# Spreading the first layer norm over the engines, and its side work over ticks, in a four-layer attention kernel

## The chip, the cores and the metric

The kernel runs on one core of one Trainium2 chip. The metric is device time in microseconds (us) of one execution. A kernel is timed several times in alternation with the kernel before on the same chip; medians are quoted ("same": within 2%).

TensorE does matmuls, ScalarE (ACT in the profile) the exps, VectorE (DVE) the masks, evictions and statistics, GpSimd (POOL) small work and stores, SyncE (SP) issues most loads.

## The reference

Four residual layers in turn: windowed attention (weights A), full attention (weights B), A again, B again. Each normalizes x first. The sequence has 2048 rows of 640 columns in bfloat16, with 32 heads of 20.

```python
x = x + _A_ref(_layernorm(x), A_wqkv, A_wo)     # window of 256 keys
x = x + _B_ref(_layernorm(x), B_wqkv, B_wo)     # all keys
x = x + _A_ref(_layernorm(x), A_wqkv, A_wo)
x = x + _B_ref(_layernorm(x), B_wqkv, B_wo)
# inside: qkv = x @ wqkv; softmax(q k^T * 20**-0.5) v; @ wo
```

## The kernel before

Work goes by chunks of 512 rows and groups of four heads. A loop over ticks emits, in each tick, scores of two or three banks, one exp group, side tasks (projections, layer norms, output projections) as far as a credit allows, the mask products of the tick before, and the products with v. Every engine gets its instructions in one order, and here a mask product that was emitted behind a side task of VectorE waited for it (the hole of 5.01 us in the prediction). So where a side task is emitted decides whom it holds up. A side task that yields `("pe", n)` spends credit and may go on in the same tick; one that yields `("wait", n)` sleeps for n ticks.

The start, with one load for the weights of q and k and all zeros of `ka` on VectorE:

```python
nc.sync.dma_start(out=raw[:], in_=wq_view[0][:, :, 0 : 2 * D])
...
nc.vector.memset(ka_all[:, G:KA, :], 0.0)
```

The layer norm of the general task, which the first chunk also used:

```python
def t_ln(l, c):
    ...                                   # waits for x; copies the first weights
    nc.gpsimd.tensor_scalar(...)          # var + eps, four row tiles at once
    nc.gpsimd.tensor_tensor(out=rstd[:], in0=rstd[:], in1=nhalf[:], op=ALU.pow)
    yield ("wait", 2)
    ...
    for i in range(4):
        nc.vector.tensor_scalar(out=xn[:], in0=x_sb[:, 4 * c + i, :], ...)
        yield ("wait", 1)
        mb = yield from take_m()          # one of two PSUM banks
        ...                               # five transposes
        evac(xt[:, :, i * P : (i + 1) * P], trp)
```

The statistics of the first layer's x, all four tiles of a chunk at once, and the zeros:

```python
def t_stats0(c):
    for i in range(4):
        stats(0, c, i)                    # two bn_stats, one bn_aggr on VectorE
        yield ("pe", 0.1)
    ready.add(("x", 0, c))

def t_zeros():
    for n in range(2):
        nc.vector.memset(wop[:, 4 * n : 4 * n + 4, :], 0.0)
        yield ("wait", 3)
    load_wop(0)
    ...                                   # kt and qt, ten pieces on VectorE
```

The weights of later projections, on SyncE's queue like the small loads of q and k:

```python
nc.sync.dma_start(out=t[:], in_=wq_view[l % 2][:, :, a : a + P])
```

The softmax here doesn't subtract the row's maximum and nothing guards it: scores larger than these inputs give would overflow.

Of the kernel before, what the change touches and what calls it, by code (L numbers as in the profile page):

```python
# [9 lines left out]
BF16 = mybir.dt.bfloat16  # L10
F32 = mybir.dt.float32
I32 = mybir.dt.int32
ALU = mybir.AluOpType
ACT = mybir.ActivationFunctionType

P = 128
S = 2048
D = 640
# [3 lines left out]
KD = D // P  # L22
G = 8
C = 512
NC = S // C
EPS = 1e-5
SCALE = DH ** -0.5
HD = D // 2
# [10 lines left out]
KA = 18  # L39
# [10 lines left out]
def kernel(  # L50
# [10 lines left out]
    nc = tc.nc  # L61
# [11 lines left out]
    xtp = pool("xtp", 5)  # L73
# [5 lines left out]
    xnp = pool("xnp", 2)  # L79
    lnp = pool("lnp", 4)  # L80
# [11 lines left out]
    x_sb = big.tile([P, NT, D], BF16, name="x_sb", tag="x_sb")  # L92
    raw = big.tile([P, KD, 2 * D], BF16, name="raw", tag="early_late")
    wv_sb = [big.tile([P, KD, D], BF16, name=f"wv{w}", tag=f"wv{w}") for w in range(2)]
    wop = big.tile([P, G, D], BF16, name="wop", tag="wop")
    ident = big.tile([P, P], BF16, name="ident", tag="ident")
    nhalf = big.tile([P, 4], F32, name="nhalf", tag="nhalf")
# [6 lines left out]
    ka_all = big.tile([P, KA, C], BF16, name="ka", tag="ka")  # L104
    kas = [ka_all[:, n, :] for n in range(KA)]
    qas = [big.tile([P, C], BF16, name=f"qa{n}", tag=f"qa{n}") for n in range(QA)]

    ps = psp.tile([P, 8, C], F32, name="ps", tag="ps")
    op = ps[:, 7, :]
# [6 lines left out]
    wq_view = [w.rearrange("(c p) f -> p c f", p=P) for w in wqkv_in]  # L116
    nc.sync.dma_start(out=x_sb[:, 0:2, :], in_=xin[:, 0:2, :])
    nc.sync.dma_start(out=x_sb[:, 2:4, :], in_=xin[:, 2:4, :])
    nc.sync.dma_start(out=raw[:], in_=wq_view[0][:, :, 0 : 2 * D])
    nc.sync.dma_start(out=wv_sb[0][:], in_=wq_view[0][:, :, 2 * D : 3 * D])  # L120
    for c in range(1, NC):
        nc.sync.dma_start(out=x_sb[:, 4 * c : 4 * c + 4, :], in_=xin[:, 4 * c : 4 * c + 4, :])
# [24 lines left out]
            base=0, pattern=[[1 if ge else -1, P]], channel_multiplier=-1 if ge else 1,  # L147
        )

    nc.vector.memset(ka_all[:, G:KA, :], 0.0)  # L150

    def other_constants():
        nc.vector.memset(op, 0.0)
# [16 lines left out]
    ready = set()  # L170
# [19 lines left out]
    def push(name, gen, need, left):  # L190
        lead = 0
        if type(name) is tuple and need <= first_use(1, NC - 1, 0):

            chain = {"out": True, "ln": name[1] == 1, "v": name[1] == 1 and name[-1] == 0}
            lead = 5 * chain.get(name[0], False)
            if name[0] in ("k", "q"):
                lead = 7 if name[1] == 1 and name[-1] == 0 else 2
        insort(todo, Task(name, gen, need, left, lead))
# [65 lines left out]
    def require(what):  # L264
        n = 0
        while what not in ready:
            n += 1
            assert n < 100000, what
            t = choose(False, state["unit"] if n < 400 else 1 << 30)
            if t is None:  # L270
                state["tick"] += 1
                continue
            state["credit"] = max(state["credit"] - advance(t), -1.0)


    live = Counter()
# [9 lines left out]
    users = {}  # L286
# [18 lines left out]
    def get_w(l, n, c, i):  # L305

        t = wqkp.tile([P, KD, P], BF16, name="wqk", tag="wqk")
        wtick[l, n, c, i] = state["tick"] + 4
        if l or c:
            a = n * D + i * P  # L310
            nc.sync.dma_start(out=t[:], in_=wq_view[l % 2][:, :, a : a + P])
            return t
        tv = t[:].rearrange("p c (j m) -> p c j m", j=4)
        nc.gpsimd.memset(tv[:, :, :, DH:32], 0.0)
        src = raw[:, :, n * D + 80 * i : n * D + 80 * (i + 1)]
        nc.vector.tensor_copy(
            out=tv[:, :, :, 0:DH], in_=src.rearrange("p c (j e) -> p c j e", j=4)
        )
        wtick[l, n, c, i] = 0
        return t  # L320
# [39 lines left out]
    def stats(l, c, i):  # L360
        if (l, c) not in mvs:
            mvs[l, c] = lnp.tile([P, 4, 2], F32, name="mv", tag="mv")
        st = lnp.tile([P, 2, 6], F32, name="stats", tag="stats")
        xv = x_sb[:, 4 * c + i, :]
        nc.vector.bn_stats(out=st[:, 0, :], in_=xv[:, 0:HD])
        nc.vector.bn_stats(out=st[:, 1, :], in_=xv[:, HD:D])
        nc.vector.bn_aggr(out=mvs[l, c][:, i, :], in_=st[:])

    def t_ln(l, c):
        while ("x", l, c) not in ready:  # L370
            yield ("wait", 1)
        yield from room("xnT", "ln")
        for n in (1, 0):
            order = worder[l, n]
            if order and not any(e in wtiles for e in order):
                wtiles[order[0]] = get_w(*order[0])
        users[l, c] = 9 if (l, c) == (0, 0) else (11, 12, 11, 11)[l]
        mv = mvs.pop((l, c))
        rstd = lnp.tile([P, 4], F32, name="rstd", tag="rstd")
        nc.gpsimd.tensor_scalar(  # L380
            out=rstd[:], in0=mv[:, :, 1], scalar1=EPS, scalar2=1.0, op0=ALU.add, op1=ALU.mult
        )
        nc.gpsimd.tensor_tensor(out=rstd[:], in0=rstd[:], in1=nhalf[:], op=ALU.pow)
        yield ("wait", 2)
        nmr = lnp.tile([P, 4], F32, name="nmr", tag="nmr")
        nc.vector.scalar_tensor_tensor(
            out=nmr[:], in0=mv[:, :, 0], scalar=-1.0, in1=rstd[:], op0=ALU.mult, op1=ALU.mult
        )
        xt = xtp.tile([P, KD, C], BF16, name="xnT", tag="xnT")
        for i in range(4):  # L390
            xn = xnp.tile([P, D], BF16, name="xn", tag="xn")
            nc.vector.tensor_scalar(
                out=xn[:], in0=x_sb[:, 4 * c + i, :],
                scalar1=rstd[:, i : i + 1], scalar2=nmr[:, i : i + 1],
                op0=ALU.mult, op1=ALU.add,
            )
            yield ("wait", 1)
            mb = yield from take_m()
            trp = ps[:, mb, :].bitcast(BF16)[:, 0 : KD * P].rearrange("p (c m) -> p c m", c=KD)
            for dc in range(KD):  # L400
                nc.tensor.transpose(  # L401
                    out=trp[:, dc, :], in_=xn[:, dc * P : (dc + 1) * P], identity=ident[:]
                )
            evac(xt[:, :, i * P : (i + 1) * P], trp)
            drop_m(mb)
            yield ("pe", 0.4)
        xnT[l, c] = xt
        live["ln"] -= 1
        ready.add(("xnT", l, c))
# [158 lines left out]
    def push_layer(l, c):  # L568

        need = [first_use(l, c, g) for g in range(G)]  # L570
        push(("ln", l, c), t_ln(l, c), need[0], 1.6)
        if l % 2:
            halves = ((0,), (1,)) if l == 1 else ((0, 1),)
            for h in halves:
                push(("v", l, c, *h), t_v(l, c, h), need[4 * h[0]], 2.8 * len(h))
        elif c or l:
            push(("v", l, c), t_v(l, c, (0, 1)), need[0], 5.6)
        if c or l:
            for b in range(KD):
                g = b * P // 80  # L580
                for n in (1, 0):
                    worder[l, n].append((l, n, c, b))
                    first = index[l, c, g, PARTS[l][0] if l % 2 and c == 0 else None]
                    first = need[g] if n else first
                    push(("qk"[n], l, c, b), t_block(l, n, c, b), first, 1.1)
            return
        for g in range(G):
            for n in (0, 1):
                worder[l, n].append((l, n, c, g))
            push(("qk", l, c, g), t_qk_first(l, c, g), need[g], 2.2)  # L590
            if g == 0:
                push(("v", l, c), t_v(l, c, (0, 1)), need[0], 5.6)
# [134 lines left out]
    def unit_needs(u):  # L727
        l, c, g = u.l, u.c, u.g
        if (l, c) == (0, 0):
            return [("qk", l, c, g)]  # L730
        k0, k1 = key_blocks(l, u.part)
        chunks = range(k0 // 4, k1 // 4)
        blocks = range(80 * g // P, (80 * g + 79) // P + 1)
        if u.windowed:
            return [(n, l, c, b) for b in blocks for n in "qk"]
        return ["kts"] + [("q", l, c, b) for b in blocks] + [
            n
            for cc in chunks
            for n in [("k", l, cc, b) for b in blocks] + [("v", l, cc, g // 4)]
        ]  # L740
# [256 lines left out]
                push_layer(l + 1, c)  # L997
    def t_zeros():

        for n in range(2):  # L1000
            nc.vector.memset(wop[:, 4 * n : 4 * n + 4, :], 0.0)
            yield ("wait", 3)
        load_wop(0)
        for t in (*kts, *qts):
            for n in range(0, t.shape[1], S // 2):
                nc.vector.memset(t[:, n : min(n + S // 2, t.shape[1])], 0.0)
                yield ("wait", 3)
        ready.add("kts")

    def t_stats0(c):  # L1010
        for i in range(4):
            stats(0, c, i)
            yield ("pe", 0.1)
        ready.add(("x", 0, c))

    with tc.manual_schedule():
        push("stats", t_stats0(0), 0, 0.4)
        push_layer(0, 0)
        push("zeros", t_zeros(), 0, 0.0)
        require(("xnT", 0, 0))  # L1020
        other_constants()
        require(("qk", 0, 0, 0))

        def narrow(u):
            return u.l == 0 or (u.l == 1 and u.part in PARTS[1][:3])
# [213 lines left out]
```

## Time and profile before

| | before |
|---|---|
| median of three runs | 2434.0 us (2425.71 to 2434.68) |
| profiled span | 2419.0 us |
| ScalarE busy, of the span | 91% |
| first exp starts | 22.74 us |
| TensorE idle, 22.74 to 425.29 us | 402.55 − 344.05 = 58.5 us |

The busy table says that ScalarE bounds the whole. Until the first exp ScalarE has hardly any work, and in layer 0 TensorE has holes, after which it runs at half clock.

### The profile page before, as it was taken

The numbers are of one execution on the slowest core, as the hardware profiler recorded it, in microseconds if no ns is written. First come the engines' busy times: TensorE is split into PE (matmuls) and PEld (weight loads), VectorE is DVE, ScalarE is ACT, GpSimd is POOL, SyncE is SP. The second block draws the span as 40 slices with busy tenths as digits, with TensorE's granted clock in tenths as the row PEclk, the third lists the DMA queues.
The fourth block names the chain that finished last, engine by engine and source line by source line (L and its number), as shares of the span: only waits on it lengthen the run. The fifth ranks groups of instructions, "written<-read, shape, count | busy, mean of one in ns | idle before, by whom it ended". The sixth has DMA issues, their size and how long they took to land.

```text
span 2419.0 us, 39979 instructions
## 1 busy us (share of the span) xinstructions
PE 2012.9 (83%) x15738; PEld 725.1 (30%) x15738; DVE 1274.5 (53%) x2472; ACT 2195.2 (91%) x1735; POOL 134.1 (6%) x278
## 2 busy tenths in 40 slices
PE   6887989888888888888888888888888788888886
PEld 2343333333332333333322333332321121112112
DVE  5676766423323344433343335352577767777776
ACT  5777878999999999999998989999999989999995
POOL 1111111010100001000010001001000000000000
PEclk9898999999989999999998989999855565556556
DMA  4223233232400124102230034022110010011000
GB/s 123 63 79 88 70 81 78 50 84 58 98 22 26 38 64 109 38 14 56 68 105 21 3 83 116 28 41 74 58 34 26 26 37 26 26 38 37 26 13 12
DMA packets 170828, 129.11 MB, mean 53 GB/s; under 512 B 115536, under 2 KB 153296, under 8 KB 170640
## 3 DMA queue, kind: packets, MB, share of 16 engines
q1 hardware_dynamic: 161904, 101.39, 16.8%
q0 software_dynamic: 8736, 25.18, 3.0%
q8 instruction: 123, 2.02, 0.4%
q14 instruction: 65, 0.53, 0.1%
HBM read 98.70 MB, written 27.79 MB: 52 GB/s over the span
## 4 chain that ended last, share of the span: by engine, by line
ACT 36%; PE 30%; issue 16%; DVE 13%; DMA 3%; SPq 2%; POOL 0%; ACTq 0%; DVEq 0%; POOLq 0%
ACT pt L1135 33%; PE ps L1115 7%; PE ps L346 6%; PE ps L1187 5%; PE ps L522 4%; PE ps L604 3%; PE ps L437 3%; ACT ka L1135 2%; DVE pt L1170 2%; DMA wqk<-in_B_wqkv_dram 1%; DVE st L297 1%; DVE on L987 1%; DVE oT L797 1%; DVE xnT L856 1%; PE ps L401 1%
## 5 line engine op out<-in xcount | busy, mean ns | idle before, releaser
L1135 ACT ACTIVATE pt<-ps 128x1536 bf16<-128x1536 f32 (+3 forms) x1586 | 2051.8, 1443 | 157.2 <-PE ps L1115 142.6
L1115 PE MATMUL ps<-qt,kt 32*128 32x512 bf16 x4004 | 642.0, 462 | 230.0 <-ACT pt L1135 173.6
L1187 PE MATMUL ps<-pt,vt 128*21 128x512 bf16 x3744 | 463.2, 453 | 16.4 <-DVE oT L797 14.6
L1115 PEld LDWEIGHTS <-kt 32*128 32x128 bf16 x4004 | 188.6, 94 | 631.7 <-issue 613.1
L1170 DVE TENSOR_TENSOR pt<-pt,masks 128x1024 bf16<-128x1024 bf16 (+5 forms) x403 | 240.7, 625 | 166.3 <-ACT pt L1135 165.3
L346 PE MATMUL ps<-xnT,wqk 128*128 128x512 bf16 x830 | 223.9, 395 | 28.2 <-DMA wqk<-in_B_wqkv_dram 14.7
L604 PE MATMUL ps<-masks,ident 128*128 128x512 bf16 x764 | 231.8, 415 | 6.8 <-DVE st L297 2.5
L1187 PEld LDWEIGHTS <-vt 128*21 128x21 bf16 x4004 | 103.3, 90 | 350.0 <-issue 338.7
L297 DVE CAST st<-ps 128x512 bf16<-128x512 f32 x127 | 87.8, 691 | 202.5 <-PE ps L346 202.1
L522 PE MATMUL ps<-wop,on 128*128 128x320 bf16 x968 | 173.1, 320 | 7.2 <-DVE x_sb L531 4.1
L987 DVE TENSOR_TENSOR on<-oT,ps 128x512 bf16<-128x512 bf16 x128 | 87.6, 684 | 111.7 <-PE ps L983 105.8
L1115 PE MATMUL ps<-qa,ka 32*128 32x384 bf16 (+2 forms) x1408 | 117.2, 278 | 30.6 <-ACT pt L1135 27.1
L531 DVE TENSOR_TENSOR x_sb<-x_sb,ps 128x320 bf16<-128x320 bf16 x120 | 58.1, 484 | 150.2 <-PE ps L522 150.1
L835 DVE TENSOR_SCALAR xnT<-ps 128x512 int32<-128x512 f32 x92 | 63.5, 691 | 128.5 <-PE ps L829 125.4
L1135 ACT ACTIVATE ka<-ps 128x2048 bf16<-128x2048 f32 x65 | 127.0, 1954 | 2.6 <-PE ps L1115 2.2
L437 PE MATMUL ps<-wv,xnT 128*128 128x320 bf16 x640 | 113.8, 311 | 7.4 <-DVE on L987 1.5
L522 PEld LDWEIGHTS <-on 128*128 128x128 bf16 x968 | 90.0, 102 | 76.4 <-issue 40.7
L346 PEld LDWEIGHTS <-wqk 128*128 128x128 bf16 x830 | 71.2, 99 | 127.1 <-issue 49.4
L797 DVE CAST oT<-ps 128x512 bf16<-128x512 f32 x112 | 76.8, 686 | 53.0 <-PE ps L1187 39.5
L604 PEld LDWEIGHTS <-ident 128*128 128x128 bf16 x764 | 67.8, 102 | 114.7 <-issue 77.5
L1187 PE MATMUL ps<-pt,va 128*21 128x384 bf16 (+2 forms) x1408 | 80.5, 294 | 23.9 <-DVE oT L797 14.4
L976 DVE COPY rT<-ps 32x128 bf16<-32x128 bf16 x128 | 26.7, 209 | 93.6 <-PE ps L974 92.9
(78 smaller groups left out, 1426.0 us busy)
## 6 DMA issues: line engine op xcount, KB each, us to landing
vt<-v_d SPq DMA_DIRECT2D x48, 336.0 KB
kt<-k_d SPq DMA_DIRECT2D x192, 80.0 KB
wqk<-in_B_wqkv_dram SPq DMA_DIRECT2D x80, 160.0 KB
wqk<-in_A_wqkv_dram SPq DMA_DIRECT2D x70, 160.0 KB
k_d<-st POOLq DMA_DIRECT2D x75, 128.0 KB, 2.2
q_d<-st POOLq DMA_DIRECT2D x75, 128.0 KB, 2.1
qt<-q_d SPq DMA_DIRECT2D x384, 20.0 KB
v_d<-vs POOLq DMA_DIRECT2D x16, 336.0 KB, 3.6
```

Of the source, the lines that this page charges most:

```text
L297: nc.vector.tensor_copy(out=out_, in_=in_)
L346: nc.tensor.matmul(pq, lhsT=wt[:, dc, :], rhs=xt[:, dc, :], start=(dc == 0), stop=(dc == KD - 1),)
L437: nc.tensor.matmul(pv, lhsT=xt[:, dc, i * P : (i + 1) * P], rhs=wv_sb[l % 2][:, dc, h * HD : (h + 1) * HD], start=(dc == 0), stop=(dc == K ...
L522: nc.tensor.matmul(yp, lhsT=on[:, g, qb * P : (qb + 1) * P], rhs=wop[:, g, i * HD : (i + 1) * HD], start=(last or g == 0), stop=(g == G - 1),)
L604: nc.tensor.matmul(ps[:, b, :], lhsT=ident[:], rhs=masks[:, 0, :], start=True, stop=True)
L797: nc.vector.tensor_copy(out=oT[:], in_=op)
L835: V.tensor_scalar(out=xi.bitcast(I32)[:, i * C : (i + 1) * C], in0=ps[:, 6, :], scalar1=SCALE * LOG2E * E23, scalar2=127.0 * E23, op0=ALU. ...
L987: nc.vector.tensor_tensor(out=on[:, g, :], in0=oT[:], in1=zb, op=ALU.mult)
L1115: nc.tensor.matmul(sp[:, i, col * P : (col + qn) * P], lhsT=u.k(kc, j), rhs=u.q(j, q0, qn), start=True, stop=True,)
L1135: nc.scalar.activation(out=pt[:, i:k, b0 * P :], in_=sp[:, i:k, b0 * P :], func=ACT.Exp, scale=SCALE,)
L1170: nc.vector.tensor_tensor(out=pt_[:, i:k, b0 * P :], in0=pt_[:, i:k, b0 * P :], in1=mv_, op=ALU.mult,)
L1187: nc.tensor.matmul(op[32 * j : 32 * j + VW, q0 * P : (q0 + qn) * P], lhsT=u.v(kc, j), rhs=pt[:, i, col * P : (col + qn) * P], start=(first ...
```

## The change

It gives the first chunk its own layer norm, tile by tile over VectorE, GpSimd, ScalarE and TensorE, in six PSUM banks of its own. Twenty matmuls whose result nobody reads run first, to raise TensorE's clock. The weights come in halves, zeros move from the start into the ticks, and the first layer's statistics are spread over ticks. Cuts are marked by dots. Not shown are the lines by which the first chunk skips the general task and the windowed layers' attention waits for the late zeros (`"kas"`).

```diff
-    nc.sync.dma_start(out=raw[:], in_=wq_view[0][:, :, 0 : 2 * D])
+    for h in range(2):
+        for n in range(2):
+            a = n * D + h * HD
+            nc.sync.dma_start(out=raw[:, :, a : a + HD], in_=wq_view[0][:, :, a : a + HD])
...
-    nc.vector.memset(ka_all[:, G:KA, :], 0.0)
+    nc.vector.memset(ka_all[:, G : G + 1, :], 0.0)
...
     def t_zeros():
+        yield ("wait", 12)
+        nc.vector.memset(ka_all[:, G + 1 : KA, :], 0.0)
+        ready.add("kas")
+        yield ("wait", 3)
...
     def t_stats0(c):
         for i in range(4):
             stats(0, c, i)
-            yield ("pe", 0.1)
+            yield ("wait", 2)
...
+    def first_ln():
+        ...
+        for n in range(20):
+            nc.tensor.matmul(ps[:, 0, :], lhsT=ident[:], rhs=ka_all[:, G, :], start=True, stop=True)
+        def scale(i):
+            ...                           # nmr on VectorE
+            x = xnp.tile([P, D], BF16, name="xn", tag="xn")      # two buffers
+            nc.scalar.activation(out=x[:], in_=x_sb[:, i, :], func=ACT.Identity,
+                                 scale=rs[i][:, 0:1], bias=m[:, 0:1])
+            ...                           # five transposes into bank 1 + i
+        for i in range(4):
+            stats(0, 0, i)
+            ...                           # rstd of this tile alone on GpSimd
+            if i > 0:
+                trs.append(scale(i - 1))
+        ...                               # evictions 0 to 2 and two weight copies on VectorE
+        nc.scalar.copy(out=xt[:, :, 3 * P : 4 * P], in_=trs[3])
```

## The prediction

> **What bounds the kernel now.** I read the busy table and the slices of the page first, then the chain of waits for the first 60 us, then the timeline up to 252 us, then busy time and granted clock in short windows.
>
> ```profile
> PE 2012.9 (83%) x15738; PEld 725.1 (30%) x15738; DVE 1274.5 (53%) x2472; ACT 2195.2 (91%) x1735; POOL 134.1 (6%) x278
> ...
> PEclk9898999999989999999998989999855565556556
> ```
>
> Over the whole 2419.0 us ScalarE is the bound, with its exps. The change touches only layer 0 of four (its last statistics end at 238.6 us), so what counts is the prologue before the first exp and the holes in the first 250 us. The chain of waits gives the prologue (start, length, what):
>
> ```profile
> 1.81 9.30 DMA raw<-in_A_wqkv_dram
> ...
> 11.98 1.12 DVE wop L1001
> ...
> 13.16 0.81 DVE xn L392 x2
> ...
> 16.29 1.30 ACT xnT L295 x2
> 17.59 0.04 issue
> 17.63 4.00 PE ps L346 x10
> ...
> 22.30 0.42 PE ps L1115 x6
> 22.71 0.02 issue
> 22.74 1.45 ACT pt L1135
> ```
>
> The first exp starts at 22.74 us. VectorE has its statistics done at 8.2 us but stands in its queue behind the copy of the first weights, which waits until 11.11 us for one 1.6 MB load; then a zeroing of `wop` runs in front of the scaling of x, which alternates with transposes and evictions over two PSUM banks; then ten projections take 4.00 us, 0.40 us each. The same matmuls later in this kernel take 1.19 us for five, 0.24 us each: these first ten run cold.
>
> The timeline shows three holes where VectorE does the statistics of a further chunk of x all at once, four row tiles of about 1.0 us:
>
> ```profile
> 52.03 0.61 PE L1187 MATMUL ps<-pt,va 128*21 128x384 bf16 x8 [5.01 <-DVE oT L797]
> ...
> 105.57 0.37 PE L1187 MATMUL ps<-pt,va 128*21 128x256 bf16 x1 [2.84 <-DVE pt L1170]
> ...
> 239.24 0.60 PE L1187 MATMUL ps<-pt,va 128*21 128x256 bf16 x6 [3.76 <-DVE pt L1170]
> ```
>
> In the brackets is the idle time before the instruction and who ended it. The releaser is a mask product or an eviction that stood behind the statistics (`bn_stats` from 46.87, 102.26 and 234.54 us). Windows of hole and aftermath (stretch, length, then busy time per engine, granted clock, DMA):
>
> ```profile
> 47.00:52.03 5.03, 0.01 (x3) 0.03 (x1) 4.84 (x14) 1.37 (x3) 0.91 (x2) 0.97 0.14 33
> 52.03:58.70 6.67, 6.67 (x36) 2.19 (x36) 4.33 (x13) 2.87 (x4) 1.16 (x4) 0.51 0.01 2
> ```
>
> ```profile
> 102.70:109.80 7.10, 1.66 (x13) 0.68 (x12) 6.14 (x18) 3.24 (x4) 2.29 (x3) 0.52 0.16 38
> 109.80:116.60 6.80, 6.74 (x59) 3.58 (x59) 5.33 (x13) 5.20 (x7) 0.00 (x0) 0.50 0.11 26
> 234.00:239.24 5.24, 1.48 (x11) 0.40 (x8) 5.10 (x16) 2.81 (x3) 1.57 (x3) 0.70 0.21 56
> 239.24:249.60 10.36, 8.61 (x55) 3.42 (x54) 6.42 (x16) 4.95 (x4) 0.00 (x0) 0.50 0.07 17
> ```
>
> After each hole the clock is at half for 6.7 to 10.4 us, with TensorE nearly full and ScalarE idle for a quarter to a half: there the cold TensorE is the bound.
>
> **What the Trainium skill says.** "TensorE: Matmul & The Clock Gate", Part 1, states that the clock is halved by default, is released after about 3.4 us of sustained activity in a free-running window and taken back after an idle window, with 426.7 ns (cold) and 215.7 ns (warm) between matmuls of 512 columns. The trace agrees: 0.43 us between the first projections, 0.24 us later, clock 0.5 after the holes. Its Part 4 says that transposes don't count as activity; here twenty transposes between 13.66 and 16.8 us left the projections cold, which agrees. "DMA: Bandwidth & Descriptors", Specifications, gives 512 B as the least transfer for line rate; the halved load has rows of 640 B, so it should not slow down (no run here shows 640 B yet). "SBUF — State Buffer", "SBUF: two separate sides", describes an exclusive lock on the port pair that VectorE and GpSimd share. GpSimd's two operations for rstd took 0.19 and 1.04 us beside `bn_stats` (235.75 us) but 0.72 and 1.36 us beside mask products (105.46 us), so in the prologue, beside `bn_stats`, I use 0.19 and 1.04.
>
> **The change part by part.**
>
> *Prologue.* The zeroing of `ka` shrinks from 10 blocks to 1 (2.19 us to about 0.25), but x lands at 4.05 us anyway, so this only brings TensorE's zeros in time. With `ident` ready at 2.7 us, the twenty unread matmuls start at about 2.75: some nine cold ones (0.43) to 6.5, then eleven at 0.22, end near 9.0. VectorE does tile 0 from 4.09 to 5.1 and tile 1 to 6.1 (1.0 us each, as before). GpSimd needs 0.19 + 1.04 + two hand-overs of 0.05, about 1.3 us per tile: rstd at 6.45, 7.75, 9.05, 10.35. GpSimd is thus the longest leg. nmr takes 0.1 and ScalarE scales 640 columns in about 0.7 (its 640-column copies: 0.65 to 0.7). Tile 3: nmr 10.5, scaled 11.25, five transposes 11.65, ScalarE's eviction 12.35. VectorE in the meantime: eviction 0 to 10.1, nmr 3 at 10.5, eviction 1 to 11.2, two weight copies of 0.35 to 11.9 (memsets on GpSimd at 10.35 to 11.0; data by 11.1 even if the quarters land no sooner than the whole did), eviction 2 to 12.6. So the projections start at 12.7 against 17.63, 4.9 us earlier. If still warm they take 2.4 instead of 4.0. TensorE has only transposes from 9.0 to 12.7, about 3.7 us, which is on the edge; I count half of the 1.6. The two evictions, first scores and exp follow as before: first exp at 17.0 give or take 0.9. **Gain 5.7.**
>
> *Statistics over ticks.* Same 1.0 us pieces, but two ticks apart (a tick is one exp group, 1.0 to 1.45 us of ScalarE, 1.9 us on average in chunk 0). One piece can delay a mask product by 1 us, too short for the clock to fall. The holes' cost: idle 5.02 + (7.10 − 1.66 =) 5.44 + 3.76 = 14.2 us; halved clock: half of the busy time in it, (6.67 + 1.66 + 6.74 + 8.61) / 2 = 11.8 us. Of the idle I count 60% (the work remains, and part of the second hole is the chain of rstd, scaling and transposes that follows in any case): 8.5. Of the clock I count 10. **Gain 18.5.**
>
> *Zeros.* Nine blocks of `ka` (2.19 × 9/10 = 1.97 us, in one instruction) and two of `wop` (1.125 each) move from the prologue into chunk 0 from tick 12 on. VectorE is busy 3.67 of 10 us in 30 to 40 us but 8.04 in 40 to 50, so some of the 4.2 us holds up masks: **loss 2.5.** The following zeroings of `kt` and `qt` come about 15 ticks later, but the first `kt` is loaded only at 169.6 us.
>
> *Given back.* Work drawn forward meets other limits. Before 96.4 us and at 187.5 us TensorE already waits for weights whose issue stands behind many small loads in SyncE's queue, which the change does not touch. I take a fifth of 21.7, some 4.7 us. Sum: 5.7 + 18.5 − 2.5 − 4.7 = **17 us**, so 2434 − 17 = **2417 us**.
>
> **The rivals.** (a) *The spread delays the layer norm.* Statistics are ready 8 ticks later, some 12 us, and norm, projections and loads wait for them. For: the queue is serial. Against: the loads of chunk 1's first keys were issued at 80.0 us already, and chunk 0's last group was evicted only at 109.1 us, so there was some 20 us of slack for a delay of 12. If it held, chunk starts would stall and the gain fall to about 6 us (2428). (b) *The next limit takes it all:* the total is set by SyncE's issue and weight loads in 60 to 200 us, so holes vanish but waits for DMA grow. For: that chain at 89.8 to 96.4 us is DMA. Then only the prologue and the clock at 240 us show, 8 to 10 us (2425). (c) *The zeroing makes a new hole:* 2 us in one piece behind a backlog of VectorE could stop TensorE over 3 us and cool it, costing some 5 us (2422). (d) *Everything comes through,* even waits in the second hole: 28 us (2406).
>
> **Range and chances.** The three runs of before spread over 9 us and the profiled one took 2420.9, so the noise is half of the effect. Range 2403 to 2431. Two per cent are 48.7 us, more than prologue (the part removable) and holes together; nothing moved costs that much either. Only an upset of the whole order of work, which is planned by ticks, could: 3% faster, 95% same, 2% slower.
>
> **What would show it.** First exp near 17 us, rstd on GpSimd every 1.3 us, projections after it at 0.22 (warm) or 0.43 (cold); no idle of TensorE over 3 us ended by VectorE near the statistics, and a clock of 1.0 in the windows after them; from 300 us on, the same work some 17 us earlier. The prediction is wrong if the lead at 300 us is under 8 or over 28 us, or if the lead is lost later: then the later schedule, not the prologue, decided.

## The result, and the profile after

The changed kernel took 2408.66 us (median of 4, 2397.25 to 2413.84) against 2434.34 us before. The ratio is 0.9896, 95% interval 0.985 to 0.9942. Ratios here are the mean time of one kernel's runs over that of the other's of the same rounds, so not quite the ratio of the medians. By the 2% rule that is "same", though the interval excludes 1. A second timing beside other experiments gave 0.9927 (0.9897 to 0.9958). The predicted 2417 us is a ratio of 0.993, and the measured time lies in the range.

The busy table of the changed kernel:

```profile
PE 2026.5 (84%) x15743; PEld 727.0 (30%) x15743; DVE 1278.8 (53%) x2485; ACT 2194.2 (91%) x1726; POOL 135.1 (6%) x284
```

The shares have hardly changed. The chain of waits shows the new start (start, length, what):

```profile
2.75 6.24 PE ps L1032 x20
...
9.35 0.58 ACT xn L1044
...
11.63 0.70 ACT xnT L1073
...
12.37 3.71 PE ps L350 x10
...
16.75 0.42 PE ps L1176 x6
...
17.19 0.80 ACT pt L1196
```

The first exp comes 22.74 − 17.19 = 5.55 us earlier. But the first leg is now the row of unread matmuls itself: the first transposes stand behind it until 8.99 us, and the third tile's scaling waits for a buffer that these transposes read. The ten projections took 3.71 us, not the 2.3 of a warm clock: the clock rose at 6.3 us and fell again at 13.1.

The timeline shows the holes that are left in chunk 0. In the brackets stands TensorE's idle time before the instruction and who ended it:

```profile
43.50 0.40 PE L1248 MATMUL ps<-pt,va 128*21 128x384 bf16 x8 [2.04 <-DVE oT L802]
...
56.84 1.12 DVE L1010 MEMSET wop<- 128x1280 uint32 x1 [0.22 <-issue]
...
57.88 0.43 DVE L369 BATCH_NORM_STATS2 stats<-x_sb 128x6 f32<-128x320 bf16 x1
...
59.42 0.28 PE L1248 MATMUL ps<-pt,va 128*21 128x256 bf16 x3 [2.15 <-DVE pt L1231]
...
63.08 0.61 PE L1248 MATMUL ps<-pt,va 128*21 128x384 bf16 x8 [2.62 <-DVE oT L802]
```

The hole of 5.01 us has become several of 2.0 to 2.6 us, one of them behind a zeroing of `wop` and the statistics of a tile together. Windows of those holes and their aftermath (stretch, length, busy time of PE, PEld, DVE, ACT, POOL with counts, granted clock, DMA):

```profile
41.46:43.50 2.04, 0.00 (x1) 0.02 (x1) 2.01 (x6) 1.35 (x3) 0.00 (x0) 1.00 0.00 0
43.50:47.30 3.80, 3.80 (x24) 1.42 (x25) 1.91 (x5) 1.45 (x3) 0.00 (x0) 0.55 0.00 0
57.27:63.08 5.81, 1.00 (x11) 0.46 (x10) 5.67 (x16) 2.87 (x6) 1.24 (x2) 0.82 0.00 0
63.08:74.60 11.52, 9.98 (x88) 5.08 (x87) 11.01 (x31) 8.54 (x12) 0.42 (x2) 0.50 0.53 101
```

So the clock still falls. But a hole of 2 us does not always bring it down: the same hole of 2.04 us stands at 40.35 us in e1 and at 41.30 us in e3, one of 2.03 us at 47.54 us in e4, and no half clock followed. In all 14 traces the clock changes only on a grid of 3.41 us. If the first 300 us of each are cut on that grid, the full-clock intervals in which TensorE was busy for under 45% were followed by half clock in 43 of 43 cases, those between 45 and 70% in 40 of 96, those above in none of 841. So the busy share of such an interval counts here, and not the hole's length alone: the hole above lay wholly in the interval from 40.45 to 43.87 us, in e1 it was split into 0.64 and 1.40 us.

Because both kernels do the same exps, I use them as a ruler: the columns of all exps are added up in order of time (2,418,688 in each trace), and the time at which the sum passes a mark is compared. "Lead" is the kernel before minus the other, us:

| exp columns done | before at | changed | e1 (same kernel) | e2 | e3 | e4 | e9 | e10 | e11 | e12 |
|---|---|---|---|---|---|---|---|---|---|---|
| 1,536 | 24.2 | 5.6 | 6.7 | 6.1 | 5.7 | −0.5 | 6.8 | 0.5 | 7.0 | 6.4 |
| 49,151 | 120.9 | 11.9 | 13.5 | −0.3 | 15.7 | 12.6 | 17.8 | 0.5 | 20.8 | 16.4 |
| 98,303 | 203.9 | 16.4 | 18.4 | −1.8 | 20.9 | 17.7 | 22.8 | 11.3 | 25.9 | 22.6 |
| 150,000 | 264.1 | 17.0 | 18.0 | −2.7 | 21.5 | 14.4 | 21.7 | 12.3 | 26.9 | 26.4 |
| 300,000 | 425.3 | 17.3 | 15.3 | −1.6 | 19.7 | 13.6 | 18.1 | 20.0 | 25.5 | 27.7 |
| 900,000 | 985.9 | 14.1 | 10.1 | −11.4 | 16.7 | 13.4 | 20.7 | 17.1 | 17.1 | 22.7 |
| all | 2394.3 | 7.9 | 7.0 | −17.7 | 16.6 | 16.6 | 18.3 | 20.8 | 17.7 | 19.2 |

All are single profiled executions, and beyond 300,000 columns they drift by 10 us either way. The first rows are comparable; the last is not better than one timed run. The profiled execution of the kernel before (2420.9 us) was faster than its timed runs beside it (2425.7 to 2434.7), which makes the leads at the end too small.

The ruler counts exps alone. At 49,151, 98,303 and 300,000 columns the changed kernel and e4 have sent 8,816, 16,000 and 5,120 fewer columns through TensorE than the kernel before, so part of their early lead is side work put off: at 0.216 us for 512 columns, as in e1's warm projections, up to 3.7, 6.7 and 2.2 us (an estimate).

### The profile page after: what moved, and what is told of

Same layout as the page of the kernel before. It is cut to its first block, busy times and chain, and to the rows that moved or that the text cites. A ratio compares the mean times of both kernels' runs of the same rounds, so it can differ in the third digit from the quotient of the medians.

```text
span 2411.7 us, 39997 instructions
## 1 busy us (share of the span) xinstructions
PE 2026.5 (84%) x15743; PEld 727.0 (30%) x15743; DVE 1278.8 (53%) x2485; ACT 2194.2 (91%) x1726; POOL 135.1 (6%) x284
## 4 chain that ended last, share of the span: by engine, by line
ACT 36%; PE 32%; issue 15%; DVE 12%; DMA 2%; SPq 1%; POOL 0%; ACTq 0%; DVEq 0%; POOLq 0%
ACT pt L1196 33%; PE ps L1176 8%; PE ps L350 6%; PE ps L1248 5%; PE ps L526 4%; PE ps L609 3%; PE ps L441 3%; ACT ka L1196 2%; DVE pt L1231 2%; DMA wqk<-in_B_wqkv_dram 1%; DVE on L992 1%; DVE st L301 1%; PE ps L405 1%; DVE oT L802 1%; DVE x_sb L535 1%
## 5 line engine op out<-in xcount | busy, mean ns | idle before, releaser
L1248 PE MATMUL ps<-pt,vt 128*21 128x512 bf16 x3744 | 466.7, 456 | 16.6 <-DVE oT L802 14.7
L1248 PE MATMUL ps<-pt,va 128*21 128x384 bf16 (+2 forms) x1408 | 80.1, 294 | 18.5 <-DVE oT L802 14.0
## 6 DMA issues: line engine op xcount, KB each, us to landing
vt<-v_d SPq DMA_DIRECT2D x48, 336.0 KB
v_d<-vs POOLq DMA_DIRECT2D x16, 336.0 KB, 3.6
```

What stands on the lines that cost most here:

```text
L1248: nc.tensor.matmul(op[32 * j : 32 * j + VW, q0 * P : (q0 + qn) * P], lhsT=u.v(kc, j), rhs=pt[:, i, col * P : (col + qn) * P], start=(first ...
```

## The experiments

All were correct. Four calls were made, on chips 11, 10, 11 and 7, so kernels of different calls are compared by their ratios; the median of before in them was 2428.55 (e1 to e4), 2429.47 (e5 to e8), 2428.78 (e9 to e11) and 2431.84 us (e12).

My theory after reading the trace was that the spread statistics carry most of the gain, that the late zeros cost part of what the prologue brings, and that the unread matmuls bring nothing. The rival was that the prologue carries it.

### e1: the changed kernel again

No edit.

> The changed kernel once more, unchanged, as the control of the three beside it. If the timed difference is real, about 25 us faster than before (ratio 0.990). If the profiled pair is nearer (2419.0 against 2411.7 us), about 8 us (ratio 0.997). In the profile I look at whether the lead of some 17 us at 300 to 500 us is partly lost between 530 and 1830 us again: if it is, that loss belongs to the order of the work; if it is not, it is chance of the free-running clock.

Measured: 2410.21 us (2401.17 to 2416.67, 6 runs), ratio 0.9927 (0.9897 to 0.9958). The gain is real, nearer 18 than 26 us, between the two cases expected. First exp at 16.07 us, with the ten projections at 2.32 us: in this execution the unread matmuls did keep the clock up. VectorE's and GpSimd's instructions stand in exactly the order of the first profile, yet the lead at the marks differs by up to 4 us. So such differences are chance between executions.

### e2: statistics together again

```diff
             stats(0, c, i)
-            yield ("wait", 2)
+            yield ("pe", 0.1)
```

> The changed kernel with the first layer's statistics of chunks 1 to 3 done at once again, everything else as changed. Theory: the spreading carries most of the gain, so the holes of TensorE of 3 to 5 us behind the statistics come back, the lead at about 300 us falls from 17 to between 5 and 8 us (the prologue's 5.5 and little more), and the time is 8 to 14 us longer than the changed kernel. Rival: the prologue carries it and the holes are given back elsewhere; then within 4 us of the changed kernel.

Measured: 2426.63 us, ratio 1.0000 (0.9967 to 1.0033). Against e1 that is 16.4 us longer, a little more than the 8 to 14 expected. The holes are back, and so is something that I had not expected to move, a wait for weights at 182 us:

```profile
45.94 0.61 PE L1248 MATMUL ps<-pt,va 128*21 128x384 bf16 x8 [5.02 <-DVE oT L802]
...
187.38 1.03 PE L350 MATMUL ps<-xnT,wqk 128*128 128x512 bf16 x2 [5.88 <-DMA wqk<-in_B_wqkv_dram]
```

The first line answers to the hole before the change, the second to the one that the kernel before has at 187.48 us (shown at e10). The lead of 6.1 us at the first exp is gone at 49,151 columns, where 5 to 8 us were expected to stay. So the prologue, the unread matmuls, the halves and the late zeros together bring nothing that the times can see, which is to within 8 us; the rival falls.

### e3: zeros early again

```diff
-    nc.vector.memset(ka_all[:, G : G + 1, :], 0.0)
+    nc.vector.memset(ka_all[:, G:KA, :], 0.0)
...
     def t_zeros():
-        yield ("wait", 12)
-        nc.vector.memset(ka_all[:, G + 1 : KA, :], 0.0)
         ready.add("kas")
-        yield ("wait", 3)
```

> The changed kernel with all zeros where they were before: ten blocks of ka at the start, wop without the wait of 12 ticks. Theory: the start gets no later, as VectorE waits for x until 4.2 us and the 2.2 us of zeroing end by 3.1 us (but TensorE's unread matmuls start some 0.5 us later), first exp at 17.2 to 17.7 us; the hole of TensorE at 57 to 63 us that the late zeroing makes, and the half clock of 13.7 us after it, go: 3 to 6 us faster than the changed kernel. Rival: the zeroing of wop then lies right behind the start in VectorE's queue and delays the first mask products: same time within 2 us.

Measured: 2402.27 us, ratio 0.9901 (0.9874 to 0.9928); against e1 7.9 us shorter by the medians and 0.0026 × 2428.55 = 6.3 us by the ratios, with intervals that overlap. First exp at 17.03 us, no later than in the first profile. But its projections were warm (2.33 us); against the profiles with warm projections and late zeros (e1, e2 and e6: 16.01 to 16.65 us) it is 0.4 to 1.0 us later, as the unread matmuls wait for the zeros until 3.65 us. The two holes of 57 to 63 us are 1.35 and 2.44 us here instead of 2.15 and 2.62:

```profile
55.37 0.28 PE L1245 MATMUL ps<-pt,va 128*21 128x256 bf16 x3 [1.35 <-DVE pt L1228]
...
59.02 0.61 PE L1245 MATMUL ps<-pt,va 128*21 128x384 bf16 x8 [2.44 <-DVE oT L802]
```

The lead at 49,151 columns is 15.7 us against 11.9 and 13.5 of the two profiles of the changed kernel, 2 to 4 us more, which alone could be chance (see e1). But all five profiles with early zeros lead by 15.6 to 20.8 us there (e3, e8, e9, e11, e12), all five with late zeros and spread statistics by 9.4 to 14.4 (first profile and e1; e5 9.4, e6 14.4, e7 12.7). The half clock around these holes stayed, 17.1 us of it. So late zeros do cost some us in the traces; the expected way (the clock) is not how. In the times the cost is not shown: e6 and e7, with late zeros, have ratios of 0.9899 and 0.9883.

### e4: only the spreading, in the kernel before

```diff
-            yield ("pe", 0.1)
+            yield ("wait", 2)
```

> The kernel before with the spreading alone. Theory: first exp at 22.7 us as before; holes near the statistics under 3 us; gain of 8 to 14 us over before, and with e2 the two parts add up to the whole. Rival: the wait for weights behind SyncE's queue at 173 to 191 us (5.5 us and a cold clock), which the changed kernel doesn't show, went because of the earlier start and not because of the spreading: then it is here again and the gain is under 6 us.

Measured: 2407.58 us, ratio 0.9923 (0.9894 to 0.9952), or 18.7 us, more than the 8 to 14 expected. First exp at 23.26 us. This one line of the change is the change, as far as the times go. The rival falls: the wait of 5.5 us for weights at 182 us is not here, though the start is as late as before. In e2, with the early start, it is. The waits for weights have not all gone: until 430 us TensorE waits 7.4 us for weights in e4 instead of 13.0, and its longest wait is now 3.2 us, for weights of A at 194.5 us.

The windows from the first exp to 300,000 exp columns say how it works. The kernel before, then the changed kernel, its second execution (e1), and e4:

```profile
22.74:425.29 402.55, 344.05 (x3095) 145.19 (x3094) 270.92 (x622) 316.79 (x337) 52.40 (x102) 0.93 0.27 72
```

```profile
17.19:408.03 390.84, 340.24 (x3085) 144.65 (x3084) 279.43 (x635) 312.67 (x327) 51.69 (x102) 0.94 0.29 77
```

```profile
16.07:410.00 393.93, 345.10 (x3084) 145.64 (x3083) 279.21 (x635) 312.99 (x327) 51.69 (x102) 0.93 0.30 78
```

```profile
23.26:411.70 388.44, 345.26 (x3085) 145.65 (x3084) 274.25 (x629) 312.70 (x327) 51.83 (x102) 0.93 0.28 74
```

TensorE is idle for 58.5, 50.6, 48.8 and 43.2 us (length minus the first busy time), while the mean clock is 0.93, 0.94, 0.93 and 0.93. In e4 and e1 the gain is idle time, and TensorE's busy time is 1 us longer than before; in the first profile it is 3.8 us shorter. So the clock gave nothing back that was there in each execution.

### e5: no unread matmuls

```diff
-        for n in range(20):
+        for n in range(0):
```

> The changed kernel without its twenty unread matmuls. Theory: they bring nothing. In the changed kernel they end at 8.99 us and hold the first transposes back until then, although tile 0 is scaled by about 7.5, and the clock falls at 13.1 us, so that only the first three or so of the ten projections run warm. Without them the transposes come sooner, the projections take 4.0 to 4.3 instead of 3.70 us, and the first exp starts at 16.4 to 17.4 us (17.19 with them); time the same within 3 us. Rival: they do warm the start, and without them the first exp comes at 18.2 us or later.

Measured: 2414.85 us (2400.13 to 2422.19), ratio 0.9930 (0.9872 to 0.9988); first exp at 17.67 us, just between theory and rival. The chain is mixed: the first transposes start at 7.13 instead of 8.99 us, but the ten projections take 4.42 us.

```profile
11.92 4.42 PE L350 MATMUL ps<-xnT,wqk 128*128 128x512 bf16 x10 [0.78 <-ACT xnT L1073]
```

Against this one profile the unread matmuls bring 0.5 us when the clock is lost on the way (first profile, 17.19) and 1.6 us when it is not (e1, 16.07). "They bring nothing" was too strong. The total cannot show it.

### e6: weights in one load

```diff
-    for h in range(2):
-        for n in range(2):
-            a = n * D + h * HD
-            nc.sync.dma_start(out=raw[:, :, a : a + HD], in_=wq_view[0][:, :, a : a + HD])
+    nc.sync.dma_start(out=raw[:], in_=wq_view[0][:, :, 0 : 2 * D])
```

> The changed kernel with the weights of layer 0 in one load again. Theory: the halves matter as the first weight copies, at 10.18 us in the changed kernel, would wait until the whole has landed, at 11.1 us in the kernel before, and the third eviction stands behind them: projections and first exp 0.5 to 1.0 us later. Rival: the halves land no earlier than the whole, as all loads share the engines: same first exp within 0.2 us. The time is the same within 3 us in both.

Measured: 2405.52 us, ratio 0.9899 (0.9848 to 0.9950). The first weight copy did wait, until 11.40 us instead of running at 10.18, but the projections started at 12.57 instead of 12.37 or 12.64 us (first profile, e1):

```profile
11.40 0.63 DVE L317 COPY wqk<-raw 128x400 bf16<-128x400 bf16 x2 [0.97 <-DMA raw<-in_A_wqkv_dram]
```

The halves, with rows of 640 B, land earlier, so the rival is wrong about that, but ScalarE's last eviction until 12.5 us hides it. The halves bring nothing here, against my 0.5 to 1.0.

### e7: the clock kept up until the projections

```diff
-        for n in range(20):
-            nc.tensor.matmul(ps[:, 0, :], lhsT=ident[:], rhs=ka_all[:, G, :], start=True, stop=True)
+        def warm(times):
+            for _ in range(times):
+                nc.tensor.matmul(...)                  # as before
+        warm(12)
...                                                     # in scale(i), behind the transposes
+            warm((4, 4, 4, 3)[i])
```

> The changed kernel with twelve unread matmuls in front instead of twenty, and 4, 4, 4 and 3 more behind the transposes of the four tiles, so that TensorE's activity lasts until the projections. Theory: the ten projections then run warm, 2.2 to 2.5 us instead of 3.70, and the first exp starts at 15.2 to 16.0 us; the time is 1 to 2 us shorter, which is less than the runs' spread. Rival: three idle microseconds are needed to lose the clock only if no transposes are in them; it was lost for another reason: projections 3.5 us or more again.

Measured: 2401.13 us, ratio 0.9883 (0.9833 to 0.9932); first exp at 16.19 us, nine recorded projections in 2.32 us:

```profile
12.75 2.32 PE L350 MATMUL ps<-xnT,wqk 128*128 128x512 bf16 x9
```

The projections were warm here and in the later e9, e11 and e12, which have the same unread matmuls (first exp 15.75 to 16.29 us). But with the twenty in a row they were warm too in e1, e2, e3, e6 and e8 (2.33 us each); of six profiles only the first was cold. And e1 and e6, at 16.07 and 16.01 us, start their exps as early as e7. So e7 agrees with its theory but does not show it: the twenty keep the clock in most executions as well. The total of four runs cannot tell 1 us.

### e8: statistics four ticks apart

```diff
-            yield ("wait", 2)
+            yield ("wait", 4)      # on top of e3
```

> e3 (all zeros early) with the statistics four ticks apart instead of two. Theory: the holes of 1.35 and 2.44 us at 54 to 59 us and of 1.5 us at 127 us come from two statistics that fall into a backlog of VectorE; further apart they go under 1 us, the half clock of 17.1 us at 55.7 and of 13.7 us at 127 us goes, and the lead at 300 us grows from 20 to 23 to 28 us. Rival: 8 ticks more of delay make the layer norm of chunk 1 late, and the chunk's start (first ka load at 80.0 us before) stalls: no gain or a loss of up to 6 us.

Measured: 2418.95 us, ratio 0.9944 (0.9887 to 1.0000), against 0.9901 of e3. The lead was 15.6 us at 49,151 columns, as in e3 (15.7), but 5.7 at 98,303 (e3: 20.9). Between them stands a new hole:

```profile
189.20 0.28 PE L1173 MATMUL ps<-qa,ka 32*128 32x128 bf16 x1 [4.58 <-DMA qa<-q_d]
```

So in this profile the delay does bite, but at the loads of a later chunk and not at chunk 1 as I expected; the timed intervals of e3 and e8 overlap. That pointed again to SyncE's queue.

### e9: early zeros and a kept clock

```diff
     nc.vector.memset(ka_all[:, G : G + 1, :], 0.0)
+    nc.vector.memset(ka_all[:, G + 1 : KA, :], 0.0)
...
     def t_zeros():
-        yield ("wait", 12)
-        nc.vector.memset(ka_all[:, G + 1 : KA, :], 0.0)
         ready.add("kas")
-        yield ("wait", 3)
...                                       # and the unread matmuls of e7
```

> The changed kernel with the zeros of ka at the start again (the first block first, so that the unread matmuls start at 2.75 us), those of wop without the wait of 12 ticks, and the unread matmuls as in e7. Theory: both gains add up, first exp at 16.0 to 16.4 us, the hole at 57 us shorter, lead at 300 us 19 to 23 us, and the time 22 to 32 us under before (ratio 0.987 to 0.991), 3 to 8 us under the changed kernel. Rival: the late part gives it back, time as the changed kernel within 3 us.

Measured: 2405.08 us, ratio 0.9906 (0.9880 to 0.9932). First exp at 15.91 us, lead at 49,151 columns 17.8 us. The early gains add up in the trace, but the time is no better than that of e3 or e7: the 3 to 8 us expected over the changed kernel are not settled by the ratios (0.9906 against 0.9927 and 0.9896).

### e10: weights from another queue, in the kernel before

```diff
-            nc.sync.dma_start(out=t[:], in_=wq_view[l % 2][:, :, a : a + P])
+            nc.gpsimd.dma_start(out=t[:], in_=wq_view[l % 2][:, :, a : a + P])
```

> The kernel before with one edit: the weight tiles of the projections are loaded from GpSimd's queue instead of SyncE's. Theory: TensorE's hole of 5.5 us at 182 us is the issue of weights behind small loads in SyncE's queue; on the other queue it goes (no wait over 2 us for wqk there), and 5 to 10 us of time with it. Rival: GpSimd's queue makes the weights stand behind the stores of k and q, which wait for projections, and new holes come: same time or slower.

The wait of the kernel before, from its timeline (SPq is SyncE's queue):

```profile
184.87 0.40 SPq L311 DMA_DIRECT2D wqk<-in_B_wqkv_dram  x1
...
187.48 2.31 PE L346 MATMUL ps<-xnT,wqk 128*128 128x512 bf16 x5 [5.53 <-DMA wqk<-in_B_wqkv_dram]
```

Measured: 2401.33 us (2398.79 to 2403.97), ratio 0.9891 (0.9872 to 0.9909), 26.5 us: this line alone is worth more than the expected 5 to 10, and no less than the whole change. TensorE's waits for weights of B over the whole run, in the summed waits (total us, times, longest us), before and in e10:

```profile
PE ps L346 <- DMA wqk<-in_B_wqkv_dram: 14.7, 8, 5.5
```

```profile
PE ps L346 <- DMA wqk<-in_B_wqkv_dram: 2.5, 4, 0.8
```

The 2.5 us waited for weights of A went entirely. SyncE's queue had not only been busy issuing: before the line above it stood still for 13.9 us until 168.69 us, waiting for stores of v, and then issued 38 loads one after another before these weights' turn came at 184.87. The lead table places the gain: 0.5 us until 49,151 columns, 10.8 more in the next 49,000, 8 more between 150,000 and 300,000. The holes behind the statistics (5.02, 2.84 and 3.76 us) are still there. Here the clock did come back too; from the first exp to 300,000 columns:

```profile
22.20:405.30 383.10, 336.02 (x3095) 143.89 (x3094) 271.66 (x622) 316.46 (x337) 104.94 (x164) 0.96 0.27 76
```

TensorE is idle for 47.1 us instead of 58.5 and busy for 336.0 instead of 344.0, and the clock is at half for 34.1 us instead of 54.6. Over the whole run the waits for weights fell from 17.2 to 2.5 us, by 14.7 of the 26.5 us; the rest is not traced to single waits.

### e11: zeros of kt and qt on GpSimd

```diff
-                nc.vector.memset(t[:, n : min(n + S // 2, t.shape[1])], 0.0)
+                nc.gpsimd.memset(t[:, n : min(n + S // 2, t.shape[1])], 0.0)      # on top of e9
```

> e9 with the zeros of kt and qt (4.0 us in ten pieces) on GpSimd instead of VectorE. Theory: these stand right in front of statistics in VectorE's queue (at 53.4 and 59.2 us in e3), so the holes at 54 to 59 us get 0.4 to 0.9 us shorter, and the time goes 1 to 4 us under e9. Rival: GpSimd's memsets hold VectorE's port or delay the stores of k and q: e9's time or slower.

Measured: 2402.14 us, ratio 0.9883 (0.9856 to 0.9910), 0.0023 below e9 with overlapping intervals: 5.6 us, if it is real. The trace agrees with it early: lead at 49,151 columns 20.8 against 17.8 us. Of the two holes of e3 the first went, the second stayed at 2.62 us:

```profile
57.26 0.61 PE L1252 MATMUL ps<-pt,va 128*21 128x384 bf16 x8 [2.62 <-DVE oT L803]
```

### e12: everything together

```diff
-            nc.sync.dma_start(out=t[:], in_=wq_view[l % 2][:, :, a : a + P])
+            nc.gpsimd.dma_start(out=t[:], in_=wq_view[l % 2][:, :, a : a + P])      # on top of e11
```

> e11 with the weight tiles on GpSimd's queue as in e10. Theory: the two gains lie in different waits (VectorE in chunks 0 to 2, SyncE's queue from 170 us on), e11's lead at 98,000 exp columns of 26 us, about the first 180 us, stays and e10's 10 us of the stretch after 121 us come on top in large part: lead at 300 us of 30 us or more, time 32 to 45 us under before (ratio 0.982 to 0.987). Rival: part of e11's lead is the same saving, as the spreading moved the weights' issue in front of the loads already; then no more than 3 us beyond e11 and e10.

Measured: 2390.05 us (2384.73 to 2402.07), ratio 0.9818 (0.9784 to 0.9851), about 44 us under before and the fastest kernel. By the 2% rule the verdict is "unclear", as the interval reaches from 1.5 to 2.2%. At its upper end it is still under every other ratio measured here, though not under the lower ends of all their intervals. The profiled execution was one of its slower ones (span 2400.4 us), with a lead of 27.7 us at 300,000 columns instead of the 30 expected. The gains of the spreading and of the queue add up in large part: by the ratios 0.0117 + 0.0109 = 0.0226 apart (e11, e10) and 0.0182 together. The difference, 0.0044, would be an overlap as the rival says, but it is no larger than the intervals allow (0.0034, 0.0027 and 0.0019 either way), so the overlap is not shown.

## Why the prediction was right or wrong

**The total** was right: 17 us predicted; 25.7 and 18 us in two timings, and a lead of 17.0 us at 150,000 exp columns (264 us; the prediction asked at 300 us). Several terms of its sum were wrong and cancelled, so that the sum came out so close is in part luck.

**Prologue, 5.7 us.** The size was right (5.55 us in the first profile, 6.1 to 6.7 in e1, e2 and e6, where the projections were warm), its working was not. The prediction took 1.04 us for GpSimd's power and made GpSimd the longest leg. With one column instead of four it took 0.58 us:

```profile
5.73 0.58 POOL L1064 TENSOR_TENSOR rstd<-rstd,nhalf 128x1 f32<-128x1 f32 x1
```

The longest leg was TensorE's own row of unread matmuls. That VectorE would move on at full speed was right. That the projections' clock was "on the edge" fits as well: cold in one of six profiles with these matmuls, warm in five. In the time this gain is not to be seen (e2).

**Zeros, loss of 2.5 us.** The direction was right by the traces (e3). The size is not settled: with the prologue the term should have left +3.2 us, and e2 shows 0.0, give or take 8 us. Rival (c) of the prediction happened in part: a hole of 2.15 us right behind a zeroing of `wop`.

**Statistics over ticks, gain of 18.5 us.** The size was right: e4 has 18.7 us by the ratio, and e2 loses 16.4. Of its two halves the one for the clock was wrong. The step that failed is "One piece can delay a mask product by 1 us, too short for the clock to fall". Pieces meet: a piece of statistics, an eviction and mask products queue up to 2.0 to 2.6 us, and the clock fell after the pairs of such holes (13.65 us of half clock from 60.93 us in the first profile, 17.07 us from 58.06 us in e1). The mean clock to 300,000 columns did not move (0.93 before, 0.93 in e4; 54.6 and 58.0 us at half), so the ten us counted for it were not there. In their place came idle time: 15.3 us less in e4, against 8.5 counted; in the two profiles of the changed kernel 7.9 and 9.7 us less. That 18.5 met 18.7 is luck.

**Given back, and rival (b).** "Which the change does not touch" was the second step that failed. The spreading moved the weights' issue in front of the small loads of SyncE's queue (weights of B at 166.44 us in e4, ahead of the loads of `qa` and `ka` from 175.15 us; at 184.87 us before), and the wait of 5.53 us at 182 us went (e4; back in e2, and in e8 a wait of 4.58 us for `qa` stands there). In e4 that saves 5.6 us of waits for weights until 430 us, part of the idle time beyond the 8.5 us counted. So rival (b), by which waits for DMA would grow, did not come: in the changed kernel TensorE waited 9.2 us for weights there instead of 13.0. The term itself has a slip: a fifth of 21.7 is 4.3 and not 4.7, and the sum is then 17.4 us. Why a delay of statistics puts these issues into another order I did not follow through the task list; shown is only that it does, in both directions.

**Third hole (235 to 239 us).** It went, but brought nearly nothing: from 98,303 to 150,000 columns the kernel before needed 60.2 us, the changed one 59.6. There TensorE's idle time is 9.9 us before and 10.4 us after, among it a wait for weights of 2.65 us at 196.6 us, which of the two only the changed kernel has. What else made up for the hole is open.

**Later loss.** The prediction called itself wrong "if the lead is lost later". From 300,000 columns to the end the two profiles of the changed kernel lose 9.4 and 8.3 us of their lead, 6.2 and 3.1 of these after 900,000; e3, with nearly the same order of work there, loses 3.1, of which 0.1 after 900,000. In that stretch the clock is at half for 741 us before, for 775 and 764 us in the changed kernel's profiles and for 754 us in e3. As VectorE's order is the same in the two and the loss is not, I take it for chance of the clock; that is argued and not shown. The timed means of e1 keep 18 us.

## What to carry to other kernels

Spread a burst of side work on an engine that others wait for, but expect the gain as idle time of the waiting engine first: two holes of 2 us close together still lost the clock here, and the largest part of it came back in e10, where the waits for weights went. Before tuning a prologue, check which queue holds the largest waits of the steady state; here one line that took the weights out of a crowded issue queue was worth as much as the whole change, and with the changed kernel's later variants it gave 1.8%. And a change that moves work between ticks also reorders the loads' issue, so look at the waits for DMA even where the change has no DMA in it.

## What the Trainium skill lacked or had wrong

- "TensorE: Matmul & The Clock Gate", the table of "Why this matters for your kernels", asks for no idle gaps over some 3 us; under "A second HAM failure mode: psum-queue depth-cycling" the page says that short idle times between groups of matmuls can make the clock go up and down too, but gives no share. Here a single hole of 2.04 us was followed by 3.4 us at half clock in one of two profiles of the same kernel. On the clock's grid of 3.41 us it fell after all 43 intervals with TensorE busy for under 45%, after 40 of 96 between 45 and 70%, and after none of 841 above.
- The same page, Part 1, says that the clock is at half by default, and warns that the records of its changes can be unreliable. One case that it does not name: the granted clock in the profile reads 1.00 from 11.92 to 16.34 us in e5, while the ten projections there took 4.42 us; the first record of a clock comes at 21.24 us, so before it the view does not show the cold state.
- "DMA: Bandwidth & Descriptors", "Issuing engines are not separate DMA queues", says that issuing from several engines saves only sequencer time, "which is usually small relative to the DMA itself". Here the weights stood in one queue behind a wait of 13.9 us for stores and then 38 loads, most of them of 0.27 to 0.5 us of issue each; moving the weights to another queue was worth 26.5 us of 2429 (e10).
- No page gives the time of GpSimd's power by size: 1.04 us for 128x4 and 0.58 us for 128x1.
